# A linear-attention block beside a squared-ReLU MLP on one core: start, weight fold and last tile rearranged

## The chip, the core and the metric

The kernel runs on one core of a Trainium2 chip. The metric is the device time of one execution in microseconds (us). Three executions of the kernel before took 145.36, 145.87 and 146.5 us; the median is 145.87. One further view, the profile, was taken from the execution that took 146.5 us.

## The reference

2048 tokens of 448 features, all in bf16. One layer norm feeds two branches, and the result is `x + attention * silu(mlp)`.

```python
xn = _layernorm(x)                       # x: 1 x 2048 x 448
# branch A: linear attention, 16 heads of 28
q, k, v = split(xn @ wqkv)               # wqkv: 448 x 1344
phi = lambda t: jnp.where(t > 0, t + 1, jnp.exp(t)) + 1e-6
kv  = einsum("bhsd,bhse->bhde", phi(k), v)
z   = sum over tokens of phi(k)
o   = einsum("bhqd,bhde->bhqe", phi(q), kv) / (phi(q) . z + 1e-6)
s   = o @ wo                             # wo: 448 x 448
# branch B
h = xn @ w1 + b1                         # w1: 448 x 1792
r = relu(h) ** 2
g = silu(r @ w2 + b2)                    # w2: 1792 x 448
out = x + s * g
```

## The kernel before

**Tiling.** The tokens are 16 tiles of 128, in four groups of four (512 tokens). The 448 features are three full chunks of 128 rows (c = 0, 1, 2) and a rest of 64 rows (c = 3). The rest is held twice, in partitions 0 to 63 and 64 to 127, so that two 64-row matmuls can run side by side, one in each half of the array. The 1792 hidden features are 14 units of 128; "H0.8" is unit 8 for token group 0. "K0.1" is the key product of tile 1 of group 0, "Q0.2" the third 128-feature piece of the queries of group 0.

**Order of work.** A small planner inside the kernel (`Program`) holds all operations. TensorE ("pe") and SyncE ("sp", which issues nearly all DMAs) run theirs strictly in the order in which the program adds them. For ScalarE ("act"), VectorE ("dve") and GpSimd ("pool") the planner chooses an order by estimated times, except that operations added while `pr.hot` is set run in the order written. PSUM banks (eight) are handed out by the planner as they come free. Each engine then runs a fixed list with semaphore waits, so a waiting instruction holds up everything behind it on its engine.

**Stages.** (1) Start: warm-up matmuls, layer norm of tiles 0 to 3, their transposes through TensorE, the first eight H units of group 0. (2) The other H, K and Q units of all groups, four at a time in `quads`; each quad runs as pairs of 64-row matmuls (`pe_four`), whose four steps take the first and third named unit, then the second and fourth, then the first pair's and the second pair's remaining rows. Tiles 4 to 15 are transposed by DMA (`dma_start_transpose`, issued by SP). (3) Token sums `A = xn^T phi(k)` (`token_sum`). (4) The fold: `fold_wv` multiplies Wv into A and keeps only the blocks of equal heads (`hmask`), `fold_wo` multiplies with Wo, giving one 448 x 448 matrix `msb`. (5) The second MLP product (`gg`), with silu; the product of the queries with `msb` (`ss4`, `s_main`); the gating, the residual and the store. The last tile (15) goes through in two column pieces (`gg_part`, `s_main` with `lo`, `hi`).

**The start in the code (lines 1211 to 1270).** Each of the tiles 0 to 3 is transposed by itself as soon as it is normalized: `x_transpose0((0,))` takes one PSUM bank for the four chunks of one tile, evicted as chunk 0 alone and then chunks 1 to 3 (`evac`, L765 on DVE, L766 on ACT). Between the transposes (L750) the first seven H units run in pieces `pe_part(units, first tile, tiles, chunks)` of 128 columns (L713). Tiles 0 and 1 get the copy of their last 64 features from GpSimd (`norm_rest`, L731), tiles 2 and 3 from DVE (`dup`, L726). Then follow the row-paired rests ("tails") of four units, the remaining pieces, unit 7 in one go (`pe_main`), and the other tails.

**Loads in the order of SP's queue.** Tokens 0, 1, 2 to 3; w_1 columns 0 to 895 in three row chunks (224 KB each); after tile 0 is normalized w_1 columns 896 to 1791 (672 KB, L1224) and the rests w_1r of units 0 to 7; after tile 1 tokens 4 to 7; wk; after the first eviction of tile 2 the w_1r of units 8 to 11 (L1271), wq, w_1r of units 12 and 13, tokens 8 to 11; then DMA transposes, tokens 12 to 15, w_2, b2, Wo, wv.

**The first quads (L1280)**: `H0.8 K0.0 H0.10 K0.1`, `H0.9 K0.2 H0.11 K0.3`, `Q0.0 H0.12 Q0.1 H0.13`.

**The fold (L814 to L882).** Four blocks of 112 features (four heads), each with four contraction chunks: 16 matmuls of 112 columns. The masked result `kvm` is stored in a frame of 512 columns that a memset (L378) has zeroed, with one more copy of 64 columns (L839). `fold_wo(c)` then makes one 128-row output chunk from the one or two 112-feature blocks that reach into it: seven matmuls of 448 columns.

Of the kernel before, what the change touches and what calls it, by code (L numbers as in the profile page):

```python
# [9 lines left out]
P = 128  # L10
# [289 lines left out]
def bass_recurrent_scan__linear_attn_block__dense_activation_squared_relu__prompt_kernel(  # L300
    nc, A_x, A_wqkv, A_wo, B_x, B_w1, B_b1, B_w2, B_b2, out
):
    with ExitStack() as es:
# [19 lines left out]
        w_o = sb("w_o", [P, 4, D], bf)  # L323
# [17 lines left out]
        kvm = sb("kvm", [P, 4, 512], bf)  # L341
# [36 lines left out]
        vset(kvm[:, :, :], 0.0, "kvm", dur=1.0)  # L378
# [52 lines left out]
        def load_w1_rows(c0, c1, lo, hi, eng, reads=()):  # L431
            lo, hi = P * lo, P * hi
            dma(
                eng, w_1[:, c0:c1, lo:hi], B_w1[c0 * P : c1 * P, lo:hi].rearrange("(c p) j -> p c j", p=P),
                [("w1u", fi, c) for fi in range(lo // P, hi // P) for c in range(c0, c1)], (c1 - c0) * 256 * (hi - lo),
                reads,
            )
# [9 lines left out]
        w1names = lambda fi: [("w1u", fi, c) for c in range(3)] + [("w1", fi // 4, 1), ("w1", fi // 4, 2)]  # L447
# [5 lines left out]
        for c in range(3):  # L453
            load_w1_rows(c, c + 1, 0, 7, "sp")

        def late_loads():
            dma(
                "sp", b2b[:, :], bass.AP(tensor=B_b2.tensor, offset=B_b2.offset, ap=[[0, P], [1, D]]), ["b2b"],
                P * D * 2,
            )  # L460
            dma("sp", w_o[0:PD, :, :], A_wo.rearrange("(c p) d -> p c d", p=PD), ["wo"], D * D * 2)
            load_k("sp", w_qkv, A_wqkv, "wv", 2 * D, 3 * D)
# [111 lines left out]
        def pe_part(us, t0, nt, cs=(0, 1, 2)):  # L574
            def f(e, _):
                last = None
                for k in cs:
                    for u in us:
                        last = u[2](e, slice(0, 128), k, k == 0, False, (t0, nt))
                return last  # L580

            need = {("xTt", t, k) for k in cs for t in range(t0, t0 + nt)} | {u[1][k] for u in us for k in cs}
            banks = [u[0] for u in us]
            add(
                "pe", f, sorted(need, key=str) + (banks if t0 or cs[0] else []), banks,
                len(us) * len(cs) * MM(128 * nt) + 0.01,
# [56 lines left out]
        for si in range(4):  # L643
            pr.alias(("xT", si), [("xTt", si, c) for c in range(4)])
# [58 lines left out]
        def hh(g, fi, full=True):  # L703
            b = Buf("H")

            def mm(e, rw, c, start, stop, part=None):
# [4 lines left out]
                if part is not None:  # L711
                    k, n = part
                    return e.matmul(  # L713
                        ps(b)[:, P * k : P * (k + n)], lhs, xT[rw, k : k + n, c, :], start=start and k == 0, stop=False,
# [8 lines left out]
            return b, reads + w1names(fi), mm, lambda: h_out(b, g, fi), 512  # L723
# [4 lines left out]
        def norm_rest(si):  # L728
# [6 lines left out]
                [("x", si), ("mv", si), ("rstd", si)], [("xnd", si)], 0.65,  # L735
            )

        def x_transpose0(tiles):
            b = Buf("T")
            nt = len(tiles)  # L740
            last_out = []

            def piece(cs, ks):
                def f(e, _):
                    last = None
                    v = ps(b)[:, :].bitcast(bf)
                    for k in ks:
                        for c in cs:
                            o = (c * nt + k - tiles[0]) * P
                            last = e.transpose(v[:, o : o + P], xn[:, k, c * P : (c + 1) * P], ident[:, :])  # L750
# [3 lines left out]
                    "pe", f, [(n, k) for k in ks for n in (("xn", "xnd") if 3 in cs else ("xn",))] + ["ident"],  # L754
                    [b], len(cs) * len(ks) * 0.057,
                )

            def evac(eng, c0, c1, ks=tiles):
                def f(e, _):
                    src = ps(b)[:, :].bitcast(bf)[:, c0 * nt * P : c1 * nt * P].rearrange(  # L760
                        "p (c k t) -> p c k t", c=c1 - c0, k=nt
                    )[:, :, ks[0] - tiles[0] : ks[-1] + 1 - tiles[0], :]
                    dst = xT[:, ks[0] : ks[-1] + 1, c0:c1, :].rearrange("p k c t -> p c k t")
# [4 lines left out]
                w = (c1 - c0) * len(ks)  # L768
                du = 0.16 + 0.105 * w if eng == "act" else 0.1 + 0.09 * w
                outs = [("xTt", k, c) for k in ks for c in range(c0, c1)]  # L770
                op = add(eng, f, [b] + last_out, outs, du)
                last_out[:] = outs[:1]
                return op
# [40 lines left out]
        def fold_wv():  # L814
            b = Buf("KV")

            def f(e, _):
                last = None
                for h in range(4):
                    for c in range(4):  # L820
                        last = e.matmul(
                            ps(b)[0:PD, h * PD : (h + 1) * PD], w_qkv[:, c, 2 * D + h * PD : 2 * D + (h + 1) * PD],
                            at[:, c, h * PD : (h + 1) * PD], start=(h == 0 and c == 0), stop=(c == 3),
# [4 lines left out]
            add("pe", f, [("at", c) for c in range(4)] + wnames("wv"), [b], 16 * 0.057)  # L828
            kd = free_ap(kvm[0:PD, 0:1, 0:PD], [[512 + PD, 4], [1, PD]])
# [3 lines left out]
                    out=kd, in0=ps(b)[0:PD, 0:D].rearrange("p (c i) -> p c i", c=4), in1=bcast(hmask[0:PD, :], 4),  # L833
                    op=ALU.mult,
                ),
                [b, "hmask", "kvm"], ["kvd"], 0.65,
            )
            add(
                "dve", lambda e, _: e.tensor_copy(kvm[0:PD, 3, D:512], kvm[0:PD, 3, 384:D]), ["kvd"], ["kve"], 0.12  # L839
# [24 lines left out]
        def fold_wo(c):  # L864
            b = Buf("M")
            hs = {0: (0, 1), 1: (1, 2), 2: (2, 3), 3: (3,)}[c]

            def f(e, _):
                last = None
                for h in hs:  # L870
                    lhs = kvm[0:PD, h, c * P : (c + 1) * P]
                    last = e.matmul(ps(b)[:, 0:D], lhs, w_o[0:PD, h, :], start=(h == hs[0]), stop=(h == hs[-1]))  # L872
                return last

            add("pe", f, ["kvd", "kvm", "wo"] + (["kve"] if c == 3 else []), [b], 0.19 * len(hs))
# [334 lines left out]

        H0 = {fi: hh(0, fi, fi >= 7) for fi in range(NF)}
        pr.hot = -100.0
        warm(36, 0.107)
# [10 lines left out]
        load_w1_rows(0, 3, 7, 14, "sp", [("xn", 0)])  # L1224
        load_w1_rests("sp")
        load_x(4, 8, "sp", [("xn", 1)])
        load_k("sp", w_qkv, A_wqkv, "wk", D, 2 * D)
        ln_stats(2)
        ln_stats(3)
        first = [H0[i] for i in range(7)]  # L1230
        piece, evac = x_transpose0((0,))
        piece((0, 1, 2, 3), (0,))
        evac("act", 0, 1)
        evac("act", 1, 4)
        pe_part(first, 0, 1, (0,))
        piece, evac = x_transpose0((1,))
        piece((0, 1, 2, 3), (1,))
        evac("act", 0, 1)
        pe_part(first, 0, 1, (1,))
        pe_part(first, 1, 1, (0,))  # L1240
        pe_part(first, 0, 1, (2,))
        evac("dve", 1, 4)
        ln_rstd(2, 3)
        ln_norm(2)
        dup(2)
        ln_rstd(3, 4)
        ln_norm(3)
        dup(3)
        pe_part(first, 1, 1, (1,))
        piece, evac = x_transpose0((2,))  # L1250
        piece((0, 1, 2, 3), (2,))
        evac("act", 0, 1)
        evac("act", 1, 4)
        pe_part(first, 1, 1, (2,))
        pe_part(first, 2, 1, (0,))
        piece, evac = x_transpose0((3,))
        piece((0, 1, 2, 3), (3,))
        evac("dve", 0, 1)
        t23 = evac("dve", 1, 4)
        pe_part(first[0:4], 2, 1, (1, 2))  # L1260
        pr.hot = None
        pe_part(first[0:4], 3, 1, (0, 1, 2))
# [108 lines left out]
```

## Time and profile before

| what | value |
|---|---|
| time, median of three (lowest, highest) | 145.87 us (145.36, 146.5) |
| the profiled execution's own time | 146.5 us |
| its span, first to last instruction | 144.5 us |
| around the span | 2.0 us |
| VectorE busy / ScalarE busy in 24.9 to 39.6 us | 14.4 / 12.1 of 14.7 us |
| first matmul on real data (L713) | 6.30 us |
| fold, first step (L821) on the chain | 0.82 us for 16 matmuls |
| fold, second step (L872) on the chain | 1.32 us for 7 matmuls |
| last DVE operation ends | 142.0 us |

How to read what follows. A line such as `PE pb L717 x8` is eight matmuls of TensorE that line 717 issues; many units share the lines 713 and 717, since they are the inner functions of `hh`. `PEld` is the loading of a matmul's stationary operand, which runs beside earlier matmuls. The duration of one matmul in a group contains its way through the array, so a stream of matmuls is faster than count times duration; what a stream costs is read from the chain of waits or from successive starts. "DMA to landing" counts from the issue by SP to the last of the 16 engines' arrival. In the chain, "issue" is time in which the engine waited for nothing that the profile shows.

### The profile page before, as it was taken

The page shows a single profiled execution, that of the slowest core. Times are in us where ns is not written, and L with a number is a line of the kernel's source. Part 1 is how long each engine was busy: PE and PEld are TensorE (multiplying, and loading weights), DVE is VectorE, ACT ScalarE, POOL GpSimd, SP SyncE. Part 2 cuts the span into 40 slices and gives each one's busy share as a digit, 9 for nine tenths or more (in the row PEclk, how much of TensorE's full clock was granted, in tenths as well). Part 3 has the DMA queues.
Part 4 walks back from the last instruction along what each step waited for, and adds up shares of the span by engine and source line. Part 5 has one row for each costly group of instructions (what it writes and reads, how often), then busy time and mean ns, then how long its engine had stood idle before and what let it go on. Part 6 is the DMA issues. An engine that isn't in the chain of part 4 may idle for free.

```text
span 144.5 us, 3001 instructions
## 1 busy us (share of the span) xinstructions
PE 138.4 (96%) x1199; PEld 78.7 (54%) x1199; DVE 94.4 (65%) x216; ACT 77.5 (54%) x149; POOL 33.3 (23%) x48
## 2 busy tenths in 40 slices
PE   7899699999999999999999999999999999999990
PEld 7785355555555555555555455546555554554590
DVE  5844987999999557748999980003511883575681
ACT  3555767887896349788978782149321131100120
POOL 2313004366000016600650000000000000399900
PEclk9999999999999999999999999999999999999999
DMA  3889689990052610000001000000598000024331
GB/s 94 255 264 288 184 153 300 326 208 13 0 102 48 116 29 0 5 0 0 0 5 36 0 5 0 0 0 18 153 188 163 11 0 0 0 68 159 101 129 56
DMA packets 16752, 12.56 MB, mean 87 GB/s; under 512 B 8356, under 2 KB 15844, under 8 KB 16740
## 3 DMA queue, kind: packets, MB, share of 16 engines
q1 hardware_dynamic: 16320, 11.48, 30.1%
q10 hardware_dynamic: 420, 0.91, 3.0%
q8 instruction: 9, 0.15, 0.4%
q14 instruction: 3, 0.02, 0.1%
HBM read 8.78 MB, written 1.90 MB: 74 GB/s over the span
## 4 chain that ended last, share of the span: by engine, by line
PE 92%; DMA 4%; ACT 1%; DVE 0%; SPq 0%; issue 0%
PE pb L717 25%; PE pb L984 20%; PE pb L1019 7%; PE pb L625 7%; PE pb L793 6%; PE pb L651 6%; PE pb L1096 6%; DMA w_1r<-in_B_w_dram 4%; PE pb L1184 3%; PE pb L1043 2%; PE pb L713 2%; PE pb L1169 1%; PE pb L665 1%; PE pb L799 1%; PE pb L872 1%; PE pb L750 1%
## 5 line engine op out<-in xcount | busy, mean ns | idle before, releaser
L717 PE MATMUL pb<-xT,w 64*128 64x512 bf16 (+1 forms) x291 | 38.7, 376 | 1.3 <-DMA w_1r<-in_B_w_dram 1.3
L684 ACT ACTIVATE r<-pb,b1f 128x512 bf16<-128x512 f32 x55 | 34.4, 692 | 5.5 <-PE pb L717 5.3
L984 PE MATMUL pb<-w,r 128*128 128x448 bf16 x154 | 30.0, 353 | 0.0
L717 PEld LDWEIGHTS pb<-xT,w 64*128 64x128 bf16 (+1 forms) x291 | 16.6, 94 | 15.6 <-ACT vep L476 1.8
L1085 POOL TENSOR_TENSOR obuf<-obuf,x_tok 128x448 bf16<-128x448 bf16 x12 | 12.1, 1039 | 49.1 <-DVE obuf L1079 49.1
L1069 ACT ACTIVATE gbuf<-gbuf 128x448 bf16<-128x448 bf16 x15 | 8.1, 571 | 28.2 <-DVE gbuf L993 28.2
L984 PEld LDWEIGHTS pb<-w,r 128*128 128x128 bf16 x154 | 14.9, 98 | 14.1 <-DVE obuf L1079 0.4
L993 DVE TENSOR_TENSOR gbuf<-pb,b2b 128x448 bf16<-128x448 f32 x11 | 6.9, 624 | 24.0 <-PE pb L984 24.0
L698 DVE TENSOR_TENSOR r<-r 128x512 bf16<-128x512 bf16 x39 | 18.5, 518 | 2.1 <-ACT r L684 2.1
L635 POOL TENSOR_TENSOR zacc<-zacc,pk 128x448 f32<-128x448 f32 x13 | 14.4, 1110 | 22.2 <-DVE pk L615 21.7
L625 PE MATMUL pb<-w_qkv,xT 64*128 64x448 bf16 x112 | 13.5, 349 | 0.0
L603 ACT ACTIVATE pk<-pb 128x448 bf16<-128x448 f32 x16 | 7.8, 541 | 7.0 <-PE pb L625 7.0
L1079 DVE TENSOR_TENSOR obuf<-pb,gbuf 128x448 bf16<-128x448 f32 (+1 forms) x17 | 9.3, 592 | 3.2 <-PE pb L1096 2.4
L467 DVE BATCH_NORM_STATS2 st<-x_tok 128x6 f32<-128x448 bf16 x16 | 9.3, 614 | 3.2 <-DMA x_tok<-in_A_x_dram 3.2
L651 PE MATMUL pb<-xT,w_qkv 64*128 64x512 bf16 x84 | 11.2, 376 | 0.0
L1019 PE MATMUL pb<-w,r 64*128 64x448 bf16 x112 | 10.8, 349 | 0.0
L717 PE MATMUL pb<-xT,w_1r 64*128 64x512 bf16 x56 | 10.7, 377 | 0.0
L615 DVE SCALAR_TENSOR_TENSOR pk<-pb,pk 128x448 bf16<-128x448 f32 x16 | 9.8, 622 | 0.4
L699 ACT ACTIVATE r<-r 128x512 bf16<-128x512 bf16 x17 | 9.9, 633 | 0.0
L793 PE MATMUL pb<-pk,xn 128*128 128x448 bf16 x48 | 9.3, 353 | 0.0
L625 PEld LDWEIGHTS pb<-w_qkv,xT 64*128 64x128 bf16 x112 | 6.4, 94 | 5.0
L1019 PEld LDWEIGHTS pb<-w,r 64*128 64x128 bf16 x112 | 6.4, 94 | 4.3
(90 smaller groups left out, 146.1 us busy)
## 6 DMA issues: line engine op xcount, KB each, us to landing
out_dram<-obuf SPq DMA_DIRECT2D x15, 112.0 KB, 1.7
w<-in_B_w_dram SPq DMA_DIRECT2D x1, 1568.0 KB, 10.0
x_tok<-in_A_x_dram SPq DMA_DIRECT2D x3, 448.0 KB, 3.8
w_qkv<-in_A_wqkv_dram SPq DMA_DIRECT2D x3, 336.0 KB, 6.7
w<-in_B_w_dram SPq DMA_DIRECT2D x3, 224.0 KB, 4.1
w<-in_B_w_dram SPq DMA_DIRECT2D x1, 672.0 KB, 5.9
pk<-rden_rows ACTq DMA_DIRECT2D x6, 112.0 KB
pk<-rden_rows SPq DMA_DIRECT2D x5, 112.0 KB
```

What stands on the lines that cost most here:

```text
L615: lambda e, _: e.scalar_tensor_tensor(out=slot, in0=ps(buf)[:, 0:n], scalar=1.0 + 1e-6, in1=slot, op0=ALU.add, op1=ALU.max),
L625: return e.matmul(ps(b)[:, 0:D], xT[rw, si, c, :], w_qkv[rw, c, D : 2 * D], start=start, stop=stop)
L635: lambda e, _: e.tensor_tensor(out=o[:, 0:D], in0=pk[:, 0, :] if i == 1 else zacc[:, :], in1=pk[:, i, :], op=ALU.add),
L651: return e.matmul(ps(b)[:, 0:512], w_qkv[rw, c, m * P : (m + 1) * P], xT[rw, 4 * g : 4 * g + 4, c, :], start=start, stop=stop,)
L684: rl = lambda e, _: e.activation(out=slot, in_=ps(b)[:, 0:512], func=AF.Relu, bias=b1f[:, fi : fi + 1])
L698: return e.tensor_tensor(out=slot, in0=slot, in1=slot, op=ALU.mult)
L699: return e.activation(out=slot, in_=slot, func=AF.Square)
L717: return e.matmul(ps(b)[:, 0:512], lhs, xT[rw, 4 * g : 4 * g + 4, c, :], start=start, stop=stop, skip_group_check=not full,)
L793: last = e.matmul(ps(b)[:, 0:D], xn[:, si, c * P : (c + 1) * P], pk[:, si, :], start=(si == 0), stop=(si == NT - 1),)
L984: last = e.matmul(ps(b)[:, 0:D], r2[:, fi, si * P : (si + 1) * P], w_2[:, fi, :], start=(fi == 0), stop=(fi == NF - 1),)
L1019: last = e.matmul(ps(bufs[si])[:, 0:D], r2[half[h], fi, si * P : (si + 1) * P], w_2[half[h], fi, :], start=(i < 2 and fi == 0), stop=(i >= ...
L1085: lambda e, _: e.tensor_tensor(out=ob, in0=ob, in1=x_tok[:, si, lo:hi], op=ALU.add),
```

## The change

Four things change together.

1. **Transposes of the first four tiles.** They are made in pairs of tiles. Tiles 0 and 1 use four PSUM banks, one for each chunk, evicted one by one (chunk 0 ACT, 1 DVE, 2 ACT, 3 ACT); tiles 2 and 3 use one bank, evicted by DVE in three operations. The H pieces have 256 columns instead of 128: six units take part 0 (tiles 0 and 1) with the chunks in turn, a seventh after the transposes of tiles 2 and 3, then part 1 follows for four units, tails, part 1 for three units, unit 7 and the last tails. Tile 2's last 64 features come from GpSimd instead of DVE.
2. **Loads and first quads.** w_1 is loaded in columns 0 to 1023 (three chunks of 256 KB), 1024 to 1535 and 1536 to 1791, the last two late, each after the first eviction of tiles 2 and 3. Tokens 4 to 7 go ahead of the rests. In the first three quads the K units stand before the H units.
3. **The fold.** Seven blocks of 64 features instead of four of 112. In the first step 28 matmuls of 64 columns, with 112 columns of Wv each; in the second step each 128-row output chunk is made from two matmuls that write its two 64-row halves. `w_o` holds seven overlapping slices of 112 rows, 56 rows apart. The memset of `kvm` and the 64-column copy are gone.
4. **The last tile** is gated in pieces of 256 and 192 columns instead of 224 and 224.

The core of the diff:

```diff
-        w_o = sb("w_o", [P, 4, D], bf)
+        w_o = sb("w_o", [PD, 7, D], bf)
-        kvm = sb("kvm", [P, 4, 512], bf)
+        kvm = sb("kvm", [PD, 7, 64], bf)
-        vset(kvm[:, :, :], 0.0, "kvm", dur=1.0)
...
         for c in range(3):
-            load_w1_rows(c, c + 1, 0, 7, "sp")
+            load_w1_rows(c, c + 1, 0, 2, "sp")
...
-            dma("sp", w_o[0:PD, :, :], A_wo.rearrange("(c p) d -> p c d", p=PD), ["wo"], D * D * 2)
+            wo = bass.AP(tensor=A_wo.tensor, offset=A_wo.offset, ap=[[D, PD], [56 * D, 7], [1, D]])
+            dma("sp", w_o[:, :, :], wo, ["wo"], 7 * PD * D * 2)
...
-        def x_transpose0(tiles):
-            b = Buf("T")
+        def x_transpose0(lo, pieces, share=()):
+            bs = [None] * 4
+            for p in pieces:
+                b = Buf("T")
+                for c in p:
+                    bs[c] = b
...
-                for h in range(4):
+                for j in range(7):
                     for c in range(4):
                         last = e.matmul(
-                            ps(b)[0:PD, h * PD : (h + 1) * PD], w_qkv[:, c, 2 * D + h * PD : 2 * D + (h + 1) * PD],
-                            at[:, c, h * PD : (h + 1) * PD], start=(h == 0 and c == 0), stop=(c == 3),
+                            ps(b)[0:PD, 64 * j : 64 * j + 64], w_qkv[:, c, 2 * D + 56 * j : 2 * D + 56 * j + PD],
+                            at[:, c, 64 * j : 64 * j + 64], start=(j == 0 and c == 0), stop=(c == 3),
...
-                for h in hs:
-                    lhs = kvm[0:PD, h, c * P : (c + 1) * P]
-                    last = e.matmul(ps(b)[:, 0:D], lhs, w_o[0:PD, h, :], start=(h == hs[0]), stop=(h == hs[-1]))
+                for i in (0, 1):
+                    j = min(2 * c + i, 6)
+                    last = e.matmul(
+                        ps(b)[64 * i : 64 * i + 64, 0:D], kvm[:, j, :], w_o[:, j, :], start=True, stop=True
+                    )
...
-        load_w1_rows(0, 3, 7, 14, "sp", [("xn", 0)])
+        ln_stats(2)
+        piece, evac = x_transpose0(0, [(0,), (1,), (2,), (3,)])
+        for c in range(4):
+            piece((c,))
+        evac("act", 0, 1)
+        load_x(4, 8, "sp", [("xn", 1)])
         load_w1_rests("sp")
-        load_x(4, 8, "sp", [("xn", 1)])
         load_k("sp", w_qkv, A_wqkv, "wk", D, 2 * D)
+        ln_rstd(2, 3)
+        evac("dve", 1, 2)
+        evac("act", 2, 3)
+        ln_stats(3)
+        ln_rstd(3, 4)
+        evac("act", 3, 4)
+        ln_norm(2)
+        norm_rest(2)
+        ln_norm(3)
+        dup(3)
+        first = [H0[i] for i in range(6)]
+        pe_part(first[0:4], 0, (0,))
+        pe_part(first[4:5], 0, (0,))
+        pe_part(first[5:6], 0, (0,))
+        pe_part(first, 0, (1,))
+        pe_part(first, 0, (2,))
+        piece, evac = x_transpose0(2, [(0, 1, 2, 3)])
+        piece((0, 1, 2, 3), (0,))
+        piece((0, 1, 2, 3), (1,))
+        evac("dve", 0, 1)
+        evac("dve", 1, 2)
+        t23 = evac("dve", 2, 4)
+        pe_part([H0[6]], 0)
+        for c in range(3):
+            pe_part([H0[i] for i in range(4)], 1, (c,))
...
-        load_w1r(2, "sp", [("xTt", 2, 0)])
+        load_w1_rows(0, 3, 2, 3, "sp", [("xTp", 2, 0)])
+        load_w1r(2, "sp")
         load_k("sp", w_qkv, A_wqkv, "wq", 0, D)
+        load_w1_rows(0, 3, 3, 4, "sp")
         load_w1r(3, "sp")
...
-        quads("H0.8 K0.0 H0.10 K0.1 H0.9 K0.2 H0.11 K0.3 Q0.0 H0.12 Q0.1 H0.13")
+        quads("K0.0 H0.8 K0.1 H0.10 K0.2 H0.9 K0.3 H0.11 Q0.0 H0.12 Q0.1 H0.13")
...
-        gg_part(15, 0, 224, False)
-        s_main(us[3], 3, True, 0, 224)
-        gg_part(15, 224, D, True)
-        s_main(us[3], 4, True, 224, D)
+        gg_part(15, 0, 256, False)
+        s_main(us[3], 3, True, 0, 256)
+        gg_part(15, 256, D, True)
+        s_main(us[3], 4, True, 256, D)
```

The removed start (lines 1223 to 1267 of the kernel before) is printed above.

## The prediction

> **What bounds the kernel now.** I read the page's shares and slices first, then the chain that ended last in order of time, TensorE's waits, the timeline of the first 20 us with each DMA's time to landing, and the groups by form.
>
> ```profile
> PE 138.4 (96%) x1199; PEld 78.7 (54%) x1199; DVE 94.4 (65%) x216; ACT 77.5 (54%) x149; POOL 33.3 (23%) x48
> ...
> PE   7899699999999999999999999999999999999990
> ...
> DMA  3889689990052610000001000000598000024331
> ```
>
> TensorE is the bound almost everywhere. Only slices 1, 2 and 5 and the tail leave it room, and slice 5 lies where DMA is busy.
>
> The chain, in order of time (start us, us, what):
>
> ```profile
> 5.50 0.44 PE pb L750 x4
> ...
> 7.22 1.72 PE pb L713 x28
> ...
> 9.50 0.47 SPq L400
> 9.96 0.04 issue
> 10.01 5.90 DMA w_1r<-in_B_w_dram
> 15.90 0.09 issue
> 15.99 1.04 PE pb L717 x8
> 17.04 0.76 PE pb L625 x8
> ...
> 98.96 0.82 PE pb L821 x16
> ...
> 102.44 1.32 PE pb L872 x7
> ...
> 140.94 0.37 ACT gbuf L1059
> ```
>
> From 15.99 to 140.94 the chain is TensorE without a gap: work taken from it there comes off the time, work added goes on. Before 15.99 the chain runs through a weight transfer. TensorE's waits (total us, times, longest) say what that costs:
>
> ```profile
> PE pb L717 <- DMA w_1r<-in_B_w_dram: 1.3, 1, 1.3
> ...
> PE pb L713 <- ACT xT L766: 0.4, 1, 0.4
> PE pb L713 <- DVE xT L765: 0.3, 1, 0.3
> ```
>
> And from the timeline and the groups by form:
>
> ```profile
> 14.05 0.60 PE L717 MATMUL pb<-xT,w_1r 64*128 64x512 bf16 x4
> ```
> ```profile
> L821 PEld LDWEIGHTS pb<-at,w_qkv 128*112 128x112 bf16 x16 | 1.0, 132 | 0.1
> ...
> L872 PEld LDWEIGHTS pb<-w_o,kvm 112*128 112x128 bf16 x7 | 0.7, 97 | 0.6
> ```
>
> The last tails of the first eight H units start at 14.05 and stream for 2x0.216, so TensorE could have gone on at 14.48. It went on at 15.99.
>
> **Start, TensorE's side.** Streaming rates from this trace: 128 columns 0.056 us a matmul, 448 columns 0.189 (14 in 2.65), 512 columns 0.216; on that line 256 columns cost 0.109. Before, the first eight units took 72 matmuls of 128 columns (4.0), 6 of 256 (0.65) and 3 of 512. After, they take 42 of 256 (4.6) and 3 of 512: equal to 0.1 us. What differs is the waits.
>
> The transposes now need tiles 0 and 1 both. Tile 1's normalization ends at 5.26+0.40=5.66, so the first pair goes at 5.72 (tile 0 alone went at 5.30). ACT began 0.35 after the last start of its group, so at 6.2; its 256-column eviction lies between the 278 ns of 128 and the 491 of 384, say 0.385. First real matmul: 6.67, against 6.30: **0.37 later**. Queued behind that wait is all of TensorE. From there, 18 matmuls (six units, three chunks) run to 8.65. Chunk 1's eviction (DVE, 6.45 to 6.75) and chunk 2's (ACT, after rstd of tile 2, to 7.6) come in time, as do the w_1 rows: now 256 KB instead of 224 each, so landing near 5.3, 7.1 and 7.8 for 5.2, 6.8 and 7.4. Tile 2's last 64 features move from a 0.18 DVE copy to GpSimd (0.65 as in L731, 7.25 to 7.9), under those matmuls; without that cover the transposes would start up to 0.65 later. Tiles 2 and 3: 8x0.056 to 9.1, one unit of 3x0.109 as filler to 9.45, DVE's first eviction 9.35 to 9.65: wait 0.25. Then 12x0.109 to 11.0; tails 0.64 (0.43 and two mode changes of 0.1, as at 11.94) to 11.6; 9x0.109 to 12.6; 3x0.216 to 13.26; tails 0.54 to **13.8**. That is 0.7 before the 14.48 of today: four groups of transposes cost more waits than two.
>
> **Start, the weights' side.** Today's landings (issue plus time to landing): w_1 columns 896 to 1791, 672 KB, 10.9; tokens 4 to 7, 13.1; main wk rows 14.2, its rest 15.6; w_1r of units 8 to 11, 15.9. From 7.4 to 10.9 the 672 KB came at 192 KB/us, from 10.9 to 14.2 another 912 KB at 276. The change lets SP wait for tile 1 (5.66) instead of tile 0 (4.98) before it issues tokens 4 to 7, the rests and wk; w_1 of units 8 to 11 (384 KB) and its w_1r wait on the eviction at 9.65, and behind that wait stand wq, w_1 of units 12 and 13, tokens 8 to 11 and the DMA transposes. Up to that w_1r, 2688 KB must land instead of 2880. From 7.75 the 1472 KB that follow the first w_1 take until 13.1 at 276 KB/us, until 15.4 at 192; the far end is today's 15.9. I take 14.9, since the new middle piece has the strided form that came at 192 and the others came at 276.
>
> K now leads each quad: 13.8+0.76=14.56 before an H step needs the late weights. So the wait is 14.9-14.56, with 0.18 to refill (1.04 against 0.86 at 15.99): 0.5 for 1.5 of today. The first quad ends at 13.8+2.84+0.5=17.15, today at 19.01: **1.85 saved**, between 2.37 (no wait) and 0.8 (landing at 15.9). The next quads need wq some 2.6 us later (670 KB at 276), about 17.5, wanted near 20: covered. K1 needs DMA transposes that land at 20.9 and 22.1 today; it wants them at 22.7 and DVE gets tokens 4 to 7 three us sooner: covered.
>
> **The fold.** First step: 16 matmuls of 112 columns become 28 of 64. Streaming would cost 28x0.029=0.82, as today. But the 112-column weight load takes 132 ns against 98 for 128 columns, and the 16 came 0.0515 apart where 112 columns should stream in 0.049: I read the load as the limit and keep 0.0515: 1.44, **+0.62** (bounds 0 and, at twice the spacing, +2.1). Second step: 7 matmuls of 0.189 (1.32) become four pairs at 0.189, as in L799, where two 64-column halves started 2 ns apart, plus two mode changes of 0.095 (85.70 to 85.98 for 0.19): 0.95, **-0.38** (bounds -0.57 and 0). Net +0.24. The Trainium skill ("TensorE: Matmul & The Clock Gate", LDWEIGHTS) states columns over 1.2 in ns for a weight load without the fast path, and the fast path for 128 weights only. By it 28 loads of 112 columns are 2.6 us and the net +1.4; 16 such loads would have been 1.5 us here, and the trace has 0.82, so the row decides. The 0.91 us memset of kvm (1.26 to 2.17) goes for nothing: DVE waits until 2.96 for tokens. w_o grows from 392 to 686 KB, 1.1 us at 276; it lands near 34 and is wanted at 102.
>
> **The end.** Pieces of 256 and 192 stream as many columns. The last ACT and DVE steps see 32 columns less: 0.37, 0.39 and 0.27 shrink by 0.03 each (448 against 224 columns: 571/357, 619/391, 480/275): **-0.09**; the wider first half ends on DVE near 141.1, before 141.3 is due.
>
> **Sum.** The profiled run took 146.5 (span 144.5, 2.0 around it): 146.5-1.85+0.24-0.09=144.8. It is the slowest of three, 0.63 over the median. A wait on a transfer is the likeliest thing to vary, and that I have counted; a third of the 0.63 I take to be elsewhere: **144.6**.
>
> **Rivals.** *The same wait, moved* (0.22): the third slice of w_1 is issued only at 9.7, and its tail pieces land at 15.9 like today. Against it: 192 KB less ahead. Gain 0.8: 145.6. *Evictions become the bound* (0.13): without today's pause ACT and DVE start the quads with eight unfinished units, and DVE is at 9 tenths from slice 6 to 12. For it: ACT took 9.6 of 12.5 us from 12.4 to 24.9 and would have to do that in 10.8; against: that still fits. Price 0.5: 145.2. *Slower: the clock opens late* (0.15). Warm-up matmuls came 0.107 apart, and so did the first transposes; at 6.30 it is 0.056 (the page's granted clock reads 9 throughout, so the spacing is the witness). TensorE rested 5.73 to 6.30 before; now it would rest 5.30 to 5.72 and 6.2 to 6.67, 0.4 us more. If the rate stays halved through the 18 matmuls and 8 transposes, 18x0.104+8x0.051=2.3: quads at 16.1, third slice issued at 12.0, its w_1r landing 16.6 or later, the first quad ends at 18.95, gain 0.07: 146.6; a longer stay goes past 147.4. It decides if the spacing at 7 us is 0.21. The same page (Part 1) gives windows of 3.4 us; by that the next chance after the present one is 9.2, which halves only the 18.
>
> **Numbers.** The forecast has 0.5; its own range is 143.7 to 145.7 (waits of 0 to 1, fold 0 to +0.6, the 0.63 in or out). About 1% is what a measurement of this kernel tells from no change: 144.41 and 147.33. Of the forecast 0.3 lies under 144.41; with crumbs of the others faster is 0.32. Slower takes 0.12: the worse half of the clock case and a weight load at twice the spacing. The rest, 0.56, is within 1%. Range 143.6 to 146.6.
>
> **What would show it.** First 256-column matmul near 6.7 at 0.109 apart; last tails done near 13.8; K before H at the first quad, then a wait on w or w_1r under 1 us; the first quad's end near 17.1; L821's successor 1.44, L872's 0.95. A landing after 16.6, halved rates after 6.7, or new waits on PSUM banks between 16 and 40 us would make it wrong.

## The result and the profile after

| | before | after |
|---|---|---|
| median of six (lowest to highest) | 145.99 us (145.36 to 146.5) | 144.03 us (143.89 to 145.07) |
| ratio, 95% interval | | 0.9886 [0.9847, 0.9926] |
| the profiled execution, its span | 146.5, 144.5 us | 144.71, 142.7 us |
| first matmul on real data | 6.30 | 6.29 |
| last tails of the first eight H units done | 14.48 | 13.47 |
| first quad ends | 19.01 | 17.48 |
| fold, first step / second step | 0.82 / 1.32 | 1.42 / 0.88 |

The changed kernel takes 1.1% less; a later repeat of it (`a_control` below) gave 0.9906 [0.9872, 0.994]. (The ratios here and below are those of the record, worked out over all runs of a set; they are not the ratios of the medians, which for this pair would be 0.9866.) The lines of the page of after that answer to those of before (busy time, then the slices):

```profile
PE 138.1 (97%) x1176; PEld 77.6 (54%) x1176; DVE 92.3 (65%) x215; ACT 76.2 (53%) x146; POOL 34.1 (24%) x49
...
PE   7999799999999999999999999999999999999992
...
DMA  4888799990556100000002000000698000024332
```

TensorE is still the bound. The second slice is full now (9 for 8); the first stays at 7, and the fifth (14.3 to 17.8 us) rose from 6 to 7 and is the soft one that remains. The chain that ended last in the profile of after, in order of time (start us, us, what):

```profile
12.21 0.29 DVE mv L470 x4
...
12.52 0.31 ACT vep L477
...
13.06 1.74 ACT r L685 x3
14.80 0.43 issue
15.22 1.04 PE pb L718 x8
16.26 0.57 PE pb L626 x6
16.83 0.65 PE pb L718 x6
17.48 0.76 PE pb L626 x8
...
97.44 1.42 PE pb L822 x28
...
101.51 0.88 PE pb L868 x8
```

L718, L626, L822 and L868 are the successors of L717, L625, L821 and L872. The same stretch in the timeline of after (start us, us, engine, what; in brackets the idle time before it and its releaser):

```profile
13.04 0.61 PE L718 MATMUL pb<-xT,w_1r 64*128 64x512 bf16 x4
...
13.49 0.92 PE L626 MATMUL pb<-w_qkv,xT 64*128 64x448 bf16 x8
...
15.22 0.82 PE L718 MATMUL pb<-xT,w 64*128 64x512 bf16 x6 [0.81 <-ACT r L685]
```

The K step (the eight matmuls of K0.0 and K0.1, which now open the quad) runs from 13.47 to 14.23. Then TensorE stands until 15.22, when the H step (H0.8 and H0.10) begins. The view names ScalarE's eviction, but that ended at 14.80 and TensorE started 0.43 later. The DMA records give the true releaser: the second w_1r transfer of units 8 to 11, issued at 10.29, landed 4.84 later, at 15.13. (Fifteen of its 16 engines were done at 13.90; one was 1.2 us late.)

```profile
L399 SPq DMA_DIRECT2D w_1r<-in_B_w_dram x1: 596/596/596, 10.3 to 10.3; - x1
...
DMA to landing us min/median/max: 4.8/4.8/4.8
```

A wait for several semaphores is put down to one of them, and a gap between the named releaser's end and the start is the sign that it was another.

**Where the 1.74 us of span went.** First quad's end 19.01 to 17.48: -1.53. From there to the first matmul of the stage before the fold (96.21 before, 94.68 after): 77.20 us in both. Fold: +0.60, -0.44, and +0.10 in the matmuls after it: +0.26. From the last matmuls to the last store's issue: 4.22 to 4.18, -0.04; the store's landing -0.03. The program's end, from the last landing to SP's last branch: 0.51 to 0.11, -0.40. Sum: -1.74. Both spans are of single executions, and that of before was the slowest of its six. `b_sp_one_more` below, which has the start of the kernel before unchanged, gives a second look at it: there w_1r landed at 15.27 instead of 15.90 and the first quad ended at 18.37 instead of 19.01. So some 0.6 of the 1.53 can be the scatter of one landing.

### The profile page after: what moved, and what is told of

Read it like the earlier page. It is cut to its first block, busy times and chain, and to the rows that moved or that the text cites. A ratio compares the mean times of both kernels' runs of the same rounds, so it can differ in the third digit from the quotient of the medians.

```text
span 142.7 us, 2954 instructions
## 1 busy us (share of the span) xinstructions
PE 138.1 (97%) x1176; PEld 77.6 (54%) x1176; DVE 92.3 (65%) x215; ACT 76.2 (53%) x146; POOL 34.1 (24%) x49
## 4 chain that ended last, share of the span: by engine, by line
PE 87%; DMA 5%; DVE 4%; ACT 2%; issue 1%
PE pb L718 26%; PE pb L982 21%; PE pb L1017 7%; PE pb L626 7%; PE pb L794 6%; PE pb L652 6%; PE pb L1094 6%; DMA x_tok<-in_A_x_dram 5%; DVE st L468 2%; PE pb L1041 2%; PE pb L1167 1%; PE pb L666 1%; ACT r L685 1%; PE pb L800 1%; PE pb L822 1%; PE pb L868 1%
## 5 line engine op out<-in xcount | busy, mean ns | idle before, releaser
L718 PE MATMUL pb<-xT,w 64*128 64x512 bf16 (+1 forms) x291 | 38.7, 376 | 0.8 <-ACT r L685 0.8
L685 ACT ACTIVATE r<-pb,b1f 128x512 bf16<-128x512 f32 x54 | 33.7, 691 | 6.2 <-PE pb L718 6.2
L718 PEld LDWEIGHTS pb<-xT,w 64*128 64x128 bf16 (+1 forms) x291 | 16.7, 94 | 15.0 <-ACT r L685 1.2
L982 PEld LDWEIGHTS pb<-w,r 128*128 128x128 bf16 x154 | 14.8, 98 | 14.3 <-issue 0.6
L636 POOL TENSOR_TENSOR zacc<-zacc,pk 128x448 f32<-128x448 f32 x13 | 14.5, 1115 | 22.0 <-DVE pk L616 17.8
L699 DVE TENSOR_TENSOR r<-r 128x512 bf16<-128x512 bf16 x39 | 17.8, 496 | 2.1 <-ACT r L685 2.1
L626 PE MATMUL pb<-w_qkv,xT 64*128 64x448 bf16 x112 | 13.5, 349 | 0.0
L1077 DVE TENSOR_TENSOR obuf<-pb,gbuf 128x448 bf16<-128x448 f32 (+2 forms) x17 | 9.3, 592 | 3.0 <-PE pb L1094 2.4
L1017 PE MATMUL pb<-w,r 64*128 64x448 bf16 x112 | 10.8, 349 | 0.0
L718 PE MATMUL pb<-xT,w_1r 64*128 64x512 bf16 x56 | 10.7, 377 | 0.0
L609 DVE TENSOR_SCALAR pk<-pk 128x448 bf16<-128x448 bf16 x16 | 6.0, 373 | 4.9 <-ACT pk L604 4.9
L626 PEld LDWEIGHTS pb<-w_qkv,xT 64*128 64x128 bf16 x112 | 6.3, 94 | 5.1
```

Of the source, the lines that this page charges most:

```text
L626: return e.matmul(ps(b)[:, 0:D], xT[rw, si, c, :], w_qkv[rw, c, D : 2 * D], start=start, stop=stop)
L636: lambda e, _: e.tensor_tensor(out=o[:, 0:D], in0=pk[:, 0, :] if i == 1 else zacc[:, :], in1=pk[:, i, :], op=ALU.add),
L685: rl = lambda e, _: e.activation(out=slot, in_=ps(b)[:, 0:512], func=AF.Relu, bias=b1f[:, fi : fi + 1])
L699: return e.tensor_tensor(out=slot, in0=slot, in1=slot, op=ALU.mult)
L718: return e.matmul(ps(b)[:, 0:512], lhs, xT[rw, 4 * g : 4 * g + 4, c, :], start=start, stop=stop, skip_group_check=not full,)
L982: last = e.matmul(ps(b)[:, 0:D], r2[:, fi, si * P : (si + 1) * P], w_2[:, fi, :], start=(fi == 0), stop=(fi == NF - 1),)
```

## The experiments

Theory after the result: the gain is the first quad's, and it takes the late weights' transfers and K's place together. Rivals: the gain comes from the transposes in pairs; or it comes from the program's end; the fold hides more or less than its 0.26. Differences are in us between medians; "before" is the kernel before, run in the same set.

**1. The late rests earlier.** In the changed kernel, and then in the kernel before:

```diff
         load_w1_rests("sp")
+        load_w1r(2, "sp")
         load_k("sp", w_qkv, A_wqkv, "wk", D, 2 * D)
...
         load_w1_rows(0, 3, 2, 3, "sp", [("xTp", 2, 0)])
-        load_w1r(2, "sp")
```
```diff
         load_w1_rests("sp")
+        load_w1r(2, "sp")
         load_x(4, 8, "sp", [("xn", 1)])
...
-        load_w1r(2, "sp", [("xTt", 2, 0)])
         load_k("sp", w_qkv, A_wqkv, "wq", 0, D)
```

> The changed kernel with one move: the two w_1r transfers of units 8 to 11 are issued right behind the other rests, ahead of wk, and no longer behind the 384 KB of w_1. Theory 'transfer': the second step of the first quad (L718) waits at 15.2 us for w_1r, whose last engine landed at 15.13 while fifteen had landed by 13.90, though the waits view names the relu of ACT. Then that step starts by 14.4 us (K step at 13.3 to 14.2), the first quad ends near 16.6 instead of 17.48, and the time falls by 0.6 to 0.9 us. Rival 'evictions': the step waits for PSUM banks that ACT's relus (last one ending 14.80) give back; then it stays at 14.85 to 15.2 and the time moves by less than 0.4 us.

> The kernel before with the same move: w_1r of units 8 to 11 issued right behind the other rests. Theory 'transfer order': the pause before 15.99 us is the late place of two 32 KB transfers in the queue. Its H units lead the quad and need nothing but w_1 and w_1r, so the quad starts near 14.5 to 14.7, and its K step then waits for the rest of wk, which lands near 15.7: some 0.8 to 1.2 us of the 1.5 come back, so that the kernel before would be within 0.6 us of the changed one without any of the change. Rival 'transposes in pairs': what the change gains at the start is its shorter TensorE sequence; then this run gains less than 0.4 us.

Measured: 145.4 against 145.74 before, 0.997 [0.9934, 1.0006], so about 1 us worse than the changed kernel; and 145.69, 0.9996 [0.9965, 1.0027]. Both theories failed. In `b_rest_early` the number of the rival (under 0.4 us) came out, but not for the rival's reason, as the waits show; its profile is that of the slowest of its ten executions (146.54). TensorE's waits (total us, times, longest), first in `a_rest_early`, then in `b_rest_early`:

```profile
PE pb L626 <- ACT r L685: 0.8, 1, 0.8
PE pb L718 <- ACT r L685: 0.3, 1, 0.3
```
```profile
PE pb L625 <- DMA w_qkv<-in_A_wqkv_dram: 0.7, 1, 0.7
PE pb L717 <- ACT r L684: 0.6, 1, 0.6
```

In `a_rest_early` the K step starts at 14.62 instead of 13.49 and the H step at 15.86. By the DMA records w_1r had landed at 11.35, but the last piece of wk landed at 14.53 (12.20 in after) and w_1 of units 8 to 11 at 15.77 (13.51). The two transfers are 32 KB each, so the price was not bytes. From one issue to the next SP needs 0.54 to 0.65 us for a transfer of 64 rows (0.78 for the first of them), and in this profile it issues without pause from 5.77 on: the four transfers behind the two were issued 1.3 to 1.6 us later than in after (0.27 of it since tile 1 was ready that much later). The Trainium skill ("DMA: Bandwidth & Descriptors", section "Issuing engines are not separate DMA queues") says that issuing from several engines saves only the sequencer's time to initiate a DMA, "which is usually small relative to the DMA itself". One issue is small here too, 0.60 us beside the 4.84 from issue to landing of the w_1r transfer above; but the issues stand in a row, and a late issue is a late landing. The landings of wk and w_1 moved by 2.3 us, which is 0.8 to 0.9 more than their issues did; what made the rest is not shown.

In `b_rest_early` the waits that stood behind the removed one came up one after the other: wk (last landing 15.85), then the evictions, the last of them on VectorE behind its work on tokens 4 to 7. Its chain:

```profile
14.39 2.20 DVE st L467 x4
16.60 0.28 DVE mv L469 x4
16.88 0.65 DVE r L698 x2
17.52 1.28 DVE xn L487 x4
18.80 0.23 DVE xn L496 x2
19.03 0.67 DVE r L689
19.70 0.05 issue
19.74 0.93 PE pb L625 x8
```

Tokens 4 to 7 landed at 14.37 there (9.98 in after). This suggests that the tokens that the change moves ahead matter too: early, their layer norm is out of the way of the quads' evictions. That part was not tried alone.

**2. The old order of loads in the changed kernel; H first in the changed kernel.**

```diff
-        load_x(4, 8, "sp", [("xn", 1)])
+        load_w1_rows(0, 3, 2, 4, "sp", [("xn", 0)])
         load_w1_rests("sp")
+        load_x(4, 8, "sp", [("xn", 1)])
...
-        load_w1_rows(0, 3, 2, 3, "sp", [("xTp", 2, 0)])
-        load_w1r(2, "sp")
+        load_w1r(2, "sp", [("xTp", 2, 0)])
...
-        load_w1_rows(0, 3, 3, 4, "sp")
```
```diff
-        quads("K0.0 H0.8 K0.1 H0.10 K0.2 H0.9 K0.3 H0.11 Q0.0 H0.12 Q0.1 H0.13")
+        quads("H0.8 K0.0 H0.10 K0.1 H0.9 K0.2 H0.11 K0.3 Q0.0 H0.12 Q0.1 H0.13")
```

> The changed kernel (transposes in pairs, K first in the quads) with the load order of the kernel before: the remaining w_1 columns (576 KB here) ahead of the rests, tokens 4 to 7 and wk. Theory 'transfer order': the rest of wk and w_1r then land near 15.5 to 16 us again, K cannot start before, the first quad ends near 18.4 to 18.9 instead of 17.48, and the time rises by 0.9 to 1.4 us, that is nearly all of what the start gained. Rival 'transposes in pairs': TensorE's sequence brought the gain, and the time rises by less than 0.4 us.

> The changed kernel with H ahead of K in the first three quads, as before. If the late weights (w_1 and w_1r of units 8 to 11, landing 13.5 to 15.1) end the wait, the K step no longer runs under it: the quad starts at 14.0 to 15.2 as a whole, ends 0.6 to 0.8 us later than the 17.48 of the changed kernel, and the time rises by 0.4 to 0.8 us. If evictions end the wait, the order of the steps hardly matters: less than 0.3 us.

> The changed kernel again, unaltered, on the chip of these runs, as what the others are compared with: 0.985 to 0.993 of the kernel before.

Measured: `a_loads_old` 144.84, 0.9958 [0.9926, 0.999]; `a_h_first` 145.61, 0.9989 [0.9962, 1.0016]; `a_control`, the changed kernel again, 144.34, 0.9906 [0.9872, 0.994]. H first costs 1.27 us against the control run beside it, more than was expected, and takes the whole gain. (The first quad ends at 18.36 in its profile, 0.88 after that of after: the 0.76 of the K step and a start 0.13 later.) Its chain and its wait:

```profile
10.31 4.99 DMA w_1r<-in_B_w_dram
15.31 0.05 issue
15.35 1.04 PE pb L718 x8
```
```profile
PE pb L718 <- DMA w_1r<-in_B_w_dram: 1.7, 1, 1.7
```

This is the first rival of the prediction, pure: the same wait of before on a slightly earlier landing. The landing alone gains next to nothing; with K in front 0.76 us of work runs during it.

The control shows how much is chance. Its chain:

```profile
13.49 1.16 ACT r L685 x2
14.65 0.05 issue
14.70 1.04 PE pb L718 x8
...
16.95 0.76 PE pb L626 x8
```

Here w_1r landed at 14.29 with no late engine, and the evictions (14.65) ended last. The first quad ended at 16.95, 0.53 before that of after; the two profiled times, 144.17 and 144.71, differ by 0.54. `a_loads_old` lies between theory and rival. Its median is 0.5 to 0.8 above those of the changed kernel (144.34, 144.03), but its one profile shows no wait of this kind (wk landed at 13.66, w_1r at 14.13, where the theory had 15.5 to 16):

```profile
13.75 0.93 PE pb L626 x8
...
16.76 0.76 PE pb L626 x8
```

Its last store landed at 141.71, as in the control. What separates these two profiled times (144.59 and 144.17) is the 0.4 us of the program's end, which experiment 5 takes up. So in this one profile the old order of loads cost nothing.

**3. Parts of the change in the kernel before.** New order of loads with K first, then K first alone:

```diff
-            load_w1_rows(c, c + 1, 0, 7, "sp")
+            load_w1_rows(c, c + 1, 0, 8, "sp")
...
-        load_w1_rows(0, 3, 7, 14, "sp", [("xn", 0)])
-        load_w1_rests("sp")
         load_x(4, 8, "sp", [("xn", 1)])
+        load_w1_rests("sp")
...
-        load_w1r(2, "sp", [("xTt", 2, 0)])
+        load_w1_rows(0, 3, 8, 12, "sp", [("xTt", 2, 0)])
+        load_w1r(2, "sp")
         load_k("sp", w_qkv, A_wqkv, "wq", 0, D)
+        load_w1_rows(0, 3, 12, 14, "sp")
...
-        quads("H0.8 K0.0 H0.10 K0.1 H0.9 K0.2 H0.11 K0.3 Q0.0 H0.12 Q0.1 H0.13")
+        quads("K0.0 H0.8 K0.1 H0.10 K0.2 H0.9 K0.3 H0.11 Q0.0 H0.12 Q0.1 H0.13")
```

> The kernel before with two parts of the change only: the new load order (w_1 columns 0 to 1023 first, tokens 4 to 7, rests, wk, then w_1 of units 8 to 11 with their w_1r late) and K ahead of H in the first three quads. Transposes one tile at a time, old fold, pieces of 224. Theory 'K under the weights': these two carry the gain; TensorE reaches the quads at 14.5, the K step runs while the late weights land (14 to 15.3), the first quad ends near 17.3, and the run is 1.0 to 1.6 us faster than the kernel before (ratio 0.989 to 0.993), as fast as the changed kernel or faster. Rival 'transposes in pairs': TensorE must be a microsecond earlier to use the weights; then at most 0.6 us are gained (0.996 or more).

> The kernel before with K ahead of H in the first three quads alone. Theory: the old load order brings the rest of wk at 15.6 and w_1r at 15.9, so K cannot start before 15.7 and the step behind it finds the weights there; 0.2 to 0.5 us are gained at the first quad at most, and the time is within 0.4 us of the kernel before. Rival: the order of the steps alone is the gain; then it is 1 us or more faster.

Measured: 144.59, 0.9906 [0.9869, 0.9943], and 145.46, 0.996 [0.9931, 0.9989], both against 145.88. The first has the old transposes, the old fold and the old last pieces, and gains what the whole change gains. Its chain:

```profile
13.47 1.19 PE pb L717 x7
14.66 0.76 PE pb L625 x8
15.41 0.86 PE pb L717 x8
16.28 0.57 PE pb L625 x6
16.84 0.65 PE pb L717 x6
17.49 0.76 PE pb L625 x8
```

TensorE reaches the quad at 14.66 and goes through without a wait; w_1r landed at 14.76, under the K step. The first quad ends at 17.49, where that of after ends at 17.48. K first alone only brings the next wait up, on wk:

```profile
PE pb L625 <- DMA w_qkv<-in_A_wqkv_dram: 1.1, 1, 1.1
```

| order of loads | first in the quad | transposes one by one (old fold) | in pairs (new fold) |
|---|---|---|---|
| old | H | 1 (before) | |
| old | K | 0.996 | 0.9958 |
| new | H | | 0.9989 |
| new | K | 0.9906 | 0.9886, 0.9906 |

The intervals reach some 0.003 to 0.004 to each side. Down the columns the gain needs both parts: 0.1% for the loads without K first, 0.4% for K first without the loads, 0.9 to 1.1% for both. One thing goes with the rows: with the old order SP has 82 instructions in the trace, with the new one 83, and by experiment 5 that can be up to 0.4 us (0.3%). Four runs of one set have 83 throughout: `b_sp_one_more` (old order, H first) 0.9983, `best1` (old order, K first, pairs, old fold) 0.9949, `a_h_first` (new order, H first) 0.9989, `a_control` (new order, K first) 0.9906. They say the same. K first is worth 1.27 us there, and the order of loads, with K first, 0.63 (144.97 to 144.34), although `best1` has the shorter fold. The share of the order is the weaker of the two: the intervals of its two runs overlap in this set as in the left column, and in the profiles with pairs and K first the end of the first quad does not tell the orders apart (16.76 and 17.57 with the old one, 16.95 to 17.58 with the new). In the left column it does, 18.53 and 17.49.

Across the rows the right-hand column, which also carries the fold's 0.26 us (0.2%), is level with the left. So the pairs are not needed for the gain; that they are worth a few tenths of a microsecond, which the fold takes back, is not excluded.

**4. The fold and the last pieces.** `a_fold_old` is the changed kernel with the fold, `kvm`, its memset and `w_o` of before; `a_224` has the old pieces:

```diff
-        w_o = sb("w_o", [PD, 7, D], bf)
+        w_o = sb("w_o", [P, 4, D], bf)
...
-                for j in range(7):
+                for h in range(4):
```
```diff
-        gg_part(15, 0, 256, False)
-        s_main(us[3], 3, True, 0, 256)
-        gg_part(15, 256, D, True)
-        s_main(us[3], 4, True, 256, D)
+        gg_part(15, 0, 224, False)
+        s_main(us[3], 3, True, 0, 224)
+        gg_part(15, 224, D, True)
+        s_main(us[3], 4, True, 224, D)
```

> The changed kernel with the fold of the kernel before (four blocks of 112, seven full matmuls, memset of kvm, 392 KB of Wo). From the two chains: L822 1.42 against 0.82, L868 0.88 against 1.32, and 0.10 more in the matmuls behind it for the change of mode. So the new fold costs 0.26 us, and this run should have the old chain (0.82, 1.32) and be 0.2 to 0.3 us faster than the changed kernel. Rival: the extra 294 KB of Wo and the memset weigh elsewhere too; then the first quad or the start of the DMA transposes moves by more than 0.2 us.

> The changed kernel with the last tile in pieces of 224 and 224. From the two chains the end costs 4.22 us from the last L1167 pair to the last DMA issue with 224, 4.18 with 256 and 192, so only 0.04 us is at stake: the last DVE operation should come 4.2 us behind the same point, and the time is that of the changed kernel within 0.3 us. With 83 SP instructions the end of the program keeps 0.1 us. Rival: the pieces carry the 0.4 us at the end; then 0.5 us pass there.

Measured: 144.66, 0.9913 [0.9876, 0.995], and 144.83, 0.9917 [0.9883, 0.9951]. Neither differs from the changed kernel by more than the intervals. The profile of `a_fold_old` has the fold 0.26 us shorter, as expected, but its median is not the lower one: the time of the whole run can't show so little. In `a_224` the last VectorE operation ends 1.10 us after the start of the last matmul, 1.01 in after, while its stream of matmuls up to there is 0.03 shorter.

**5. The program's end.** The 0.51 or 0.11 us between the last store's landing and SP's last branch goes with the number of SP's instructions in the profiles: 0.49 to 0.51 in the four kernels with 82 (before, `b_rest_early`, `a_loads_old`, `b_k_first`), 0.11 to 0.12 in the nine with 83. It is in the device time of these executions too, which runs 2.88 to 2.92 us past the last store's landing in the four and 2.46 to 2.57 in the nine. `b_sp_one_more` is the kernel before with the load of b2 in two halves, one SP instruction more:

```diff
-            dma(
-                "sp", b2b[:, :], bass.AP(tensor=B_b2.tensor, offset=B_b2.offset, ap=[[0, P], [1, D]]), ["b2b"],
-                P * D * 2,
-            )
+            pr.alias("b2b", [("b2b", 0), ("b2b", 1)])
+            for i in (0, 1):
+                dma(
+                    "sp", b2b[:, 224 * i : 224 * i + 224],
+                    bass.AP(tensor=B_b2.tensor, offset=B_b2.offset + 224 * i, ap=[[0, P], [1, 224]]), [("b2b", i)], P * D,
+                )
```

> The kernel before with the load of b2 in two halves, so that SP has 83 instructions in the trace instead of 82. Observation: in the profiles of the kernel before and of two of its relatives with 82 SP instructions, 0.47 to 0.51 us pass between the landing of the last store and SP's last branch; in the changed kernel and two relatives with 83 it is 0.09 to 0.1. Theory 'end of program': the 0.4 us go with SP's number of instructions, and the changed kernel gains them by its one load more. Then this run has 0.1 us there and is 0.3 to 0.45 us faster than the kernel before. Rival: the 0.4 us belong to the last tile's pieces of 256 and 192; then this run keeps 0.5 us and the time of the kernel before.

Measured: 145.49 against 145.52, 0.9983 [0.9956, 1.0009]. In its profile the end is 0.11, as predicted by the count, with the old pieces of 224: the rival of the pieces is out. The medians do not settle what it is worth: the interval, -0.64 to +0.13 us, holds both -0.40 and nothing. Why the count should matter is open.

**6. Two tries at a faster version.** `best1` is `a_loads_old` with the first w_1 load cut in two and the old fold; `best2` is the changed kernel with the old fold and the w_1r of units 8 to 11 issued by GpSimd, early and off SP's queue:

```diff
-        load_w1_rows(0, 3, 2, 4, "sp", [("xn", 0)])
+        load_w1_rows(0, 3, 2, 3, "sp", [("xn", 0)])
+        load_w1_rows(0, 3, 3, 4, "sp")
```
```diff
         norm_rest(1)
+        load_w1r(2, "pool")
...
-        load_w1r(2, "sp")
```

> The changed kernel with the load order of the kernel before (late w_1 columns ahead of the rests, tokens 4 to 7 and wk), but those columns in two transfers so that SP keeps 83 instructions, and with the old fold. If the parts add up as the profiles show (old load order: second MLP product starts at 37.39 instead of 37.89; old fold 0.26 to 0.33; end of program 0.1 instead of 0.5), it is 0.6 to 0.9 us faster than the changed kernel, 0.98 to 0.985 of the kernel before. If the start of the old load order was luck of one profile, it is 0.2 to 0.4 us faster than the changed kernel.

> The changed kernel with the old fold, and with the two w_1r transfers of units 8 to 11 issued from GpSimd behind its second normalization (near 5.8 us), where SP spends 1.2 us on them. If SP's issue time and a late last engine are what is left of the wait (w_1r lands by 11, w_1 of units 8 to 11 by 13.9), the second step of the first quad starts by 14.7 in every run, and the kernel is 0.3 to 0.8 us faster than the changed one (ratio to before 0.984 to 0.988). If the evictions (14.65 to 14.80 in two profiles) are the next bound, only the fold's 0.26 us and the scatter between runs are gained (0.987 to 0.990). If GpSimd's descriptors delay its third normalization, the transposes of tiles 2 and 3 start later than 8.5 and it is slower.

Measured: 144.97, 0.9949 [0.9922, 0.9976], and 144.98 (144.22 to 145.66), 0.9927 [0.9892, 0.9962]. Both missed what was expected of them. `best1` waits 1.0 us for wk at the K step (landed at 14.47; 13.66 in `a_loads_old`, which has the same order). `best2`'s profile does what was hoped:

```profile
12.61 1.19 PE pb L718 x7
13.79 0.76 PE pb L626 x8
14.55 0.86 PE pb L718 x8
```

w_1r landed at 10.5, no wait is left at the first quad, which ends at 16.63, and the profiled execution took 144.22. The other executions went up to 145.66, and why is open; no trace of a long one exists. Part of the gain goes at the program's end (81 SP instructions). Only 0.10 us lie between the last store's landing and SP's last branch, but 0.49 from there to the drain behind it (0.19 in after), and in all eight executions 2.16 to 2.25 us lie outside the span (1.91 to 1.97 in the control). So the last store landed 0.59 before that of the control (141.12 and 141.71), and the profiled times are level (144.22 and 144.17). No version clearly better than the changed kernel was found.

## Why the prediction was right, and where it was not

The time, 144.03, lies in the range and 0.57 under the forecast of 144.6. That the profiled execution took 144.71 where the sum had 144.8 is luck in part: the first quad saved 0.32 less than forecast, and the program's end, which was not in the sum, gave 0.40. The ratio sits on the 1% line, where the prediction gave 0.32 to faster and 0.56 to within 1%.

- **First real matmul:** 6.67 forecast, 6.29 measured. Tile 1 was normalized at 5.48, since its tokens landed at 3.42 against 3.80 in the profile of before, and ACT began 0.32 after the first transposes instead of 0.48, since these came 0.056 to 0.066 apart and not 0.107 as in before. In the control, where the tokens landed at 3.80 and the transposes came 0.107 apart, it was 6.59. The spacing was 0.109 from the first matmul on as forecast, there too; the rival of the late clock did not occur.
- **Last tails:** 13.8 forecast, 13.47 measured. From the first matmul to there 7.18, forecast 7.13: that stretch cost what was assumed, and the difference is the earlier first matmul.
- **The wait at the H step** was the mis-sized term. Forecast 0.5 (landing 14.9); in after the landing was 15.13 and the wait with its refill 17.48-13.47-2.84=1.17. Saved: 1.53 instead of 1.85. In the control the landing was 14.29 and 19.01-16.95=2.06 was saved. The forecast lies between the two; the term's own scatter was not in it.
- **What the time is due to.** The 0.7 us by which TensorE would reach the quad sooner (1.0 measured) was counted as part of the gain. `b_loads_k_first` arrives at 14.66 instead of 13.47 and ends the quad at the same time, 17.49 and 17.48. In after, the lead over the weights is spent waiting for them; in the control, where they landed early, 0.54 of it is kept. The sum came out since it was made on the landing; the credit to the transposes holds only for an early landing, and no time shows it.
- **"The same wait, moved"** was right in its mechanism and held in part: 15.13 instead of 15.90. `a_h_first` is the case in full. **"Evictions become the bound"** was close too: in the control they end 0.36 after the weights, in after 0.33 before them. (In the page of before, VectorE reads 9 tenths in slices 8 to 13, not 6 to 12.) The slices from 16 to 40 us show no new wait.
- **The fold:** +0.62 and -0.38 forecast, +0.60 and -0.44 measured, with +0.10 for the mode change ahead of the matmuls that follow, forecast with the second step: +0.26 for +0.24. The estimate from the Trainium skill ("TensorE: Matmul & The Clock Gate", section "LDWEIGHTS (loading the stationary operand)") was 2.6 us for 28 loads of 112 columns one behind the other; they came 1.42/28=0.051 us apart. The row of before held as the price of the stream and the rule did not.
- **The end:** -0.04 for -0.09 (and -0.03 at the store's landing). The program's end (-0.40) was not in the sum at all. Without it the profiled 144.71 would have been 145.1.
- **The median:** a third of the 0.63 between before's profiled run and its median was put elsewhere. The medians of before in the later sets were 145.52 to 145.88 and 145.99 in the first; the step can't be judged closer than that.

Shown: K first and the new order of loads together make the gain, without the pairs, the fold or the last pieces. That K first is needed for it is clear; that the order is needed rests on differences of 0.6 to 0.9 us between runs whose intervals overlap, and on the profiles with the old transposes. Shown in profiled executions only: the fold's +0.26 and the end's -0.40. Open: how much of the -0.40 is in the medians, and so in the gain of the new order, which brings the 83rd SP instruction with it; the long executions of `best2`; and why the old order's landings of wk differ as they do, 13.66 in `a_loads_old` and 14.47 in `best1`.

## What to carry to other kernels

When an engine waits for a transfer, list the next two or three releasers with their times before pricing the removal: here wk, the evictions and tokens 4 to 7 stood right behind the wait, and each edit of one of them alone gained 0 to 0.4 us where the right pair gained 1.3. Count a start's DMAs by the issue time of their queue as well as by their bytes, and put in front of a late operand the work that needs an operand that is already there.

## What the hardware showed that was not expected

- **A fetch of instructions, and one engine late.** In the DMA records of every profile of this study a 16 KB packet of instructions starts somewhere between 10.8 and 13.4 us (it took 0.95 us in after, 1.25 in before). Of the transfers in progress, most then have fifteen of the 16 engines done and the last 0.3 to 1.4 us later: w_1r 13.90 and 15.13 in after, 14.09 and 15.31 in `a_h_first`; a rest of wk 11.83 and 13.21 in `b_loads_k_first`. The packet's place moves from run to run. In the control it came at 13.31, w_1r was through at 14.29, and wq (15.76 and 16.34) took the delay instead. That the late engine is the one that moved the packet is inferred from the times, since the records name no engine; and a last engine 0.8 us late is seen without it as well (w_1r 9.41 and 10.21 in `best2`, whose packet started at 13.34). The landing of w_1r, 15.13 or 14.29, makes the 0.5 us between two profiles of the same kernel: their H steps start at 15.22 and 14.70.
- **SP's issue is a resource.** By successive starts in after, 0.54 to 0.65 us for a transfer of 64 rows (0.78 for the first); the first loads of tokens and of w_1 took 0.45 to 0.48. The issue beside that packet takes 1.1 to 1.7 (13.37 to 14.50 in after).
- **The last 0.4 us** of the span come and go with a single SP instruction in the thirteen profiles of experiment 5, 0.49 to 0.51 with 82 and 0.11 to 0.12 with 83.
